# An adaptive-LayerNorm block with sliding attention: the order of work in the first group of tokens

## The chip, the core and the metric

The kernel runs on one core of a Trainium2 chip. The core has five engines with a queue each: TensorE (PE, matrix multiplication; its weight loads are shown as PEld), VectorE (DVE), ScalarE (ACT), GpSimd (POOL) and SyncE (SP), which issues transfers here. An engine works through its queue in order, and an instruction waits for the semaphores of those that it depends on. The metric is the device time of one execution, in microseconds (us).

## What is computed

A block with batch 1, 2048 tokens of 448 features, 16 heads of 28 features, and attention over a window of 256 tokens. `c` gives six vectors by way of `w_mod` (shift, scale and gate for each half).

```python
mod = (_silu(c) @ w_mod).reshape(c.shape[0], 6, 1, -1)     # sa, ca, ga, sb, cb, gb
h = _layernorm(x) * (1 + ca) + sa
q, k, v = (h @ wqkv), split over 16 heads
scores = einsum("bhqd,bhkd->bhqk", q, k) * (Dh ** -0.5)
mask = (idx[:, None] - idx[None, :] >= 0) & (idx[:, None] - idx[None, :] < 256)
o = softmax(where(mask, scores, -1e9)) @ v
x = x + ga * (o @ wo)
h = _layernorm(x) * (1 + cb) + sb
x = x + gb * (mish(h @ w1 + b1) @ w2)
```

All is in float32. The kernel writes each operand of its large products as a high part, rounded to TensorE's faster format (float32r), and a remainder, and adds the products of high with high, high with remainder and remainder with high (`passes`, L183): 11 matmuls for a projection tile of 448 features.

## The kernel before

**Groups and tiles.** The tokens are worked through in four groups of 512. For a group the projections give seven tiles of 128 features for queries and keys (`qk` tiles 0 to 6: queries are features 0 to 447, keys 448 to 895, so tile 3 holds the last queries and the first keys) and four tiles of 128 tokens for values (`v0` to `v3`). Head h has its queries at feature 28h and its keys at 448 + 28h: heads 0 and 1 of group 0 need tiles 0 and 3, heads 2 and 3 need tile 4 as well, head 4 is the first that needs tile 1, head 6 the first that needs tile 5.

**A qk tile's way.** After its 11 matmuls ScalarE copies the high part out of PSUM into a tile `st` (`hi` in `qk_out`, L314), VectorE writes the remainder beside it (`lo`, L317), and SP stores both to a scratch tensor `scr` in DRAM in two transfers, 512 KB and 256 KB (four smaller ones for tile 3, which is cut at the border between queries and keys; `put`, L322). From there `L(i)` (L563) loads the queries and keys of one head, 84 rows each, as `q` and `k`. A value tile is copied to `v` by ScalarE and VectorE in the same way (`v_out`, L331).

**Attention of a head.** `A(i, t)` (L572) forms the scores of 128 queries in the tile `sA`, and VectorE adds the mask and takes the row maxima (`mx`, L581). `M2` (L585) transposes the maxima of a pair of heads (`mt`), and SP writes them as two further rows into `q` (`q<-mr`). `B` (L601) computes scores less maxima (`sB`), of which ScalarE takes the exponential twice (`P`, `Ph`); GpSimd subtracts for the remainder `Pl` (`SP`, L626), and `PV` (L632) multiplies with `v`. `EV`, `E`, `E2` and `E3` transpose and divide.

**What sets the order.** The program is written out by hand under a manual schedule: the order of the Python calls is the order on every queue. At the start (L365 to L407) the first group is normalised and transposed, ScalarE splits the weights in three sets of columns `QCOLS` (tiles 0, 3, 4; values; tiles 1, 2, 5, 6), with the remainders on GpSimd, VectorE and GpSimd, and tiles 0, 3 and 4 are formed together, in three rounds that follow the chunks of the transposed input as these come. Then come constants on GpSimd (L412 to L439): the mask, `fdf`, the fixed columns of `V`, and the rows 64 to 85 of the six `k` buffers. L899 to L916 are the lead of the attention: the loads of heads 0 to 3, all four value tiles with tiles 1 and 5 on the way, the load of head 4, and then the maxima of heads 0 to 2, with pieces of tiles 2 and 6 and the next group's normalisation between them. The loop from L919 runs three units per head: each has a piece of `B`, of `PV` and of `A` three heads ahead, the load of a head five ahead, and a share of the other work (`fill_main`, L836: the rest of the projections and the next group's), measured out by `RATE` (L872). `fill_side` (L855) is worked off one step a unit: the next group's normalisation, then the gate and the weights `wo`.

Of the kernel before, what the change touches and what calls it, by code (L numbers as in the profile page):

```python
# [8 lines left out]
F32 = mybir.dt.float32  # L9
# [42 lines left out]
def adaln_block(ctx: ExitStack, tc: tile.TileContext, x, wqkv, wo, w1, b1, w2, c, w_mod, out):  # L52
# [4 lines left out]

    def dma(o, i):
        nc.sync.dma_start(o, i)
# [11 lines left out]
    mid, mid_s = pool("mid")  # L71
    vp, vp_s = pool("vp")
    st0, st0_s = pool("st0")
    vq, vq_s = pool("vq", side="right")
# [232 lines left out]

    def qk_out(g, m, p, st=None):
        st = st or qk.tile([128, 2, GT], F32R, name=f"st{g}_{m}", tag="qs", bufs=3)
        r0, gs = m * 128, slice(g * GT, (g + 1) * GT)  # L310
        qn = min(max(D - r0, 0), 128)

        def hi():
            ACT.activation(st[:, 0], p, AF.Copy)  # L314

        def lo():
            DVE.tensor_tensor(st[:, 1], p, st[:, 0].bitcast(F32), op=ALU.subtract)  # L317

        def store():
            later.append(put)  # L320

        def put():  # L322
            for a, b, pa, ph in ((0, qn, 0, 2), (qn, 128, 1, 0)):
                if a < b:
                    dma(scr[r0 + a:r0 + b, pa:pa + 2, gs], st[a:b].bitcast(F32))
                    dma(scr[r0 + a:r0 + b, ph, gs], st[a:b, 0].bitcast(F32))
            done.add((g, m))

        return hi, lo, store
# [18 lines left out]
    def gen_qkv(g, tiles):  # L348
        first = {"v2": ("sB", 2), "v3": ("sB", 2), 1: ("pv", 1), 5: ("tr", 1)} if g == 0 else {}
        for m in tiles:  # L350
            p = bank(*first.get(m, ("mm", 2)), f"qk{g}_{m}")
            if isinstance(m, str):
# [46 lines left out]
    for lo_n, hi_n in ((0, 3), (3, 6), (6, 11)):  # L399
        for m, p, ps in first:  # L400
            for n in range(lo_n, hi_n):
                PE.matmul(p, ps[n][1], ps[n][0], start=(n == 0), stop=(n == 10))  # L402
# [8 lines left out]
    identr = att.tile([128, 128], BF16, name="identr")  # L411
    mask = att.tile([128, 384], F32, name="mask")  # L412
# [3 lines left out]
    POOL.affine_select(mask, mask, pattern=[[-1, 384]], compare_op=ALU.is_ge, fill=NEG, base=W,  # L416
                       channel_multiplier=1)
    fdf = att.tile([128, 512], F32, name="fdf", tag="P", bufs=3)
    POOL.memset(fdf[:, 0:256], 0.0)
# [4 lines left out]
    fdmask = att.tile([128, 256], BF16, name="fdmask")  # L424
    for v in V:
        POOL.memset(v[:, :, 28:29].bitcast(F32), 1.0)
        POOL.memset(v[:, :, 29:32].bitcast(F32), 0.0)
    Q2 = [att.tile([86, 2, GT], F32R, name=f"q2_{i}") for i in range(NQ // 2)]
    Q3 = [Q2[i // 2][:, i % 2] for i in range(NQ)]
    K3 = []  # L430
    for i in range(NK):
        t = att.tile([86, GT + W], F32R, name=f"k3_{i}")
        POOL.memset(t[64:86, :].bitcast(F32), -1.0)
        K3.append(t)
    O2 = []
# [435 lines left out]

    RATE = {0: 0.48, 1: 0.88, 2: 0.88, 3: 0.62}  # L872
    FRONT = {0: 0, 1: 2, 2: 2, 3: 2}
# [17 lines left out]
    def load_slot(i):  # L891
# [5 lines left out]
        L(i)  # L897

    for i in range(LEAD + 1):  # L899
        load_slot(i)  # L900
    need({f"v{t}" for t in range(4)}, 0)
    load_slot(LEAD + 1)
    DVE.tensor_copy(identr, ident)
    DVE.tensor_copy(fdmask, fdf[:, 0:256])
    for i in range(LEAD):
        for t in range(4):
            A(i, t)
            if t % 2:
                pipe.step()
                next(fillers[0])  # L910
                flush()
            side_step(0)
        if i % 2:
            pipe.step()
            next(fillers[0])
            M2(i // 2)  # L916
    NU = 3 * NS
    credit = 0.0
    for u in range(NU + 9):  # L919
# [27 lines left out]
        if g < NG:  # L947
# [21 lines left out]
        if 0 <= u - 2 < NU:  # L969
            PV(u - 2, Ph)  # L970
    for st in (FW["s2"], att_s, vp_s):
        st.close()
# [94 lines left out]
```

## Time and profile before

| what | value |
|---|---|
| median of 3 runs (lowest, highest) | 746.62 us (741.92, 748.72) |
| the profiled execution | 747.11 us |
| its span, from the first to the last instruction | 745.3 us |
| mean granted TensorE clock over the span | 0.982 of full speed |
| busy: PE, PEld | 697.2, 592.7 us |
| busy: DVE, ACT, POOL | 374.4, 388.6, 329.7 us |
| transfers | 83.86 MB, mean 113 GB/s |

A row of the timeline reads: start, time, engine, line, operation, result<-operands, shapes, count, and in brackets how long the engine had been idle before and what ended that. `SPq` is SP's queue, where a row is the issue of a transfer, not the transfer. A row of the stages reads: the stretch, its length, for each engine the busy time and the number of instructions, then the granted TensorE clock, the share of the transfer engines and GB/s. A row of the waits reads: who waited at which line for whom, the sum in us, how often, and the longest.

### The profile page before, as it was taken

To read this page: it belongs to the slowest core of one execution; us is meant where nothing else is said; L and a number is where in the kernel's file an instruction comes from. 1 tells how busy PE (TensorE), PEld (TensorE's weight loads), DVE (VectorE), ACT (ScalarE), POOL (GpSimd) and SP (SyncE) were. 2 spreads that over 40 slices of the span, in tenths; PEclk is the share of its full clock that TensorE was granted. 3 is DMA by queue.
4 is the path that set the end of the run, shared out by engine and by line. 5 is a ranking of instruction groups with operands and counts; after the bars stand their busy time and mean duration, and the time that the engine had idled before them with its cause. 6 is when DMAs were issued, how large, how long until landed. Compare 5 with 4: busy or idle time off the path is not lost.

```text
span 745.3 us, 11923 instructions
## 1 busy us (share of the span) xinstructions
PE 697.2 (94%) x3969; PEld 592.7 (80%) x3969; DVE 374.4 (50%) x1009; ACT 388.6 (52%) x740; POOL 329.7 (44%) x358
## 2 busy tenths in 40 slices
PE   3988979999999999999989889999999999999996
PEld 3766768789779887888878678888888888888885
DVE  4768645586755587664558923242323232413113
ACT  4416767676767675766868694334223222332221
POOL 4714787677656585676768865431100000000000
PEclk9898999999999999999999999999999999999999
DMA  8667643264374364453466246510200020001001
GB/s 215 201 223 230 169 152 111 84 209 148 114 219 129 99 220 144 127 156 118 133 203 207 64 147 189 139 47 1 100 0 1 1 99 1 1 0 50 1 0 50
DMA packets 48121, 83.86 MB, mean 113 GB/s; under 512 B 6126, under 2 KB 26108, under 8 KB 48060
## 3 DMA queue, kind: packets, MB, share of 16 engines
q1 hardware_dynamic: 48060, 83.10, 36.5%
q8 instruction: 32, 0.52, 0.3%
q14 instruction: 29, 0.24, 0.1%
HBM read 53.45 MB, written 29.36 MB: 111 GB/s over the span
## 4 chain that ended last, share of the span: by engine, by line
PE 80%; DVE 7%; DMA 5%; issue 3%; ACT 3%; POOL 1%; SPq 0%; DVEq 0%; ACTq 0%; POOLq 0%
PE z L812 19%; PE pv L640 9%; PE qk L294 7%; PE acc L989 6%; PE acc L990 6%; PE acc L988 6%; PE sA L579 5%; PE wo L294 5%; PE qk_v L294 5%; PE sB L609 4%; PE sB L620 3%; DMA k<-scr 2%; DVE junk L581 2%; PE qk L402 1%; PE et L651 1%
## 5 line engine op out<-in xcount | busy, mean ns | idle before, releaser
L630 POOL TENSOR_TENSOR Pl<-P,Ph 128x512 fp32r<-128x512 f32 (+2 forms) x192 | 235.7, 1234 | 99.4 <-ACT Ph L624 64.4
L581 DVE CUSTOM_DVE_ANT_0 junk<-sA,mask 128x384 f32<-128x384 f32 (+2 forms) x256 | 135.1, 528 | 120.6 <-PE sA L579 117.2
L623 ACT ACTIVATE P<-sB 128x512 f32<-128x512 f32 (+2 forms) x192 | 109.8, 572 | 62.1 <-PE sB L620 60.0
L820 DVE TENSOR_TENSOR al<-t,ah 128x512 fp32r<-128x512 f32 x56 | 38.8, 692 | 198.4 <-ACT ah L819 198.4
L818 ACT ACTIVATE t<-z,b1c 128x512 f32<-128x512 f32 x56 | 38.6, 689 | 177.2 <-PE z L812 166.3
L579 PE MATMUL sA<-k,q 84*128 84x384 f32 (+2 forms) x256 | 102.2, 403 | 10.0 <-DMA k<-scr 4.9
L624 ACT ACTIVATE Ph<-sB 128x512 fp32r<-128x512 f32 (+2 forms) x192 | 109.3, 569 | 0.0
L812 PE MATMUL z<-hhf,w 128*128 128x512 f32 x224 | 89.4, 399 | 0.0
L812 PE MATMUL z<-hlf,w 128*128 128x512 f32 x224 | 88.7, 396 | 0.0
L640 PE MATMUL pv<-Ph,v 128*60 128x256 f32 (+2 forms) x352 | 77.6, 294 | 6.9 <-ACT o L645 6.6
L988 PE MATMUL acc<-w2h,ah 128*128 128x448 f32 x224 | 82.2, 367 | 0.0
L989 PE MATMUL acc<-w2l,ah 128*128 128x448 f32 x224 | 82.0, 366 | 0.0
L990 PE MATMUL acc<-w2h,al 128*128 128x448 f32 x224 | 81.9, 366 | 0.0
L609 PE MATMUL sB<-q,k 86*128 86x256 f32 (+1 forms) x352 | 75.4, 288 | 4.4 <-DMA q<-mr 3.7
L640 PE MATMUL pv<-Pl,v 128*60 128x256 f32 (+2 forms) x352 | 74.4, 286 | 1.3 <-POOL Pl L630 1.0
L609 PEld LDWEIGHTS sB<-q,k 86*128 86x128 f32 x352 | 62.4, 192 | 6.6 <-DMA q<-mr 2.6
L812 PE MATMUL z<-hhf,w1l 128*128 128x512 f32 x168 | 66.4, 395 | 0.0
L640 PEld LDWEIGHTS pv<-Ph,v 128*60 128x60 f32 x352 | 45.4, 134 | 23.3 <-ACT o L645 10.3
L579 PEld LDWEIGHTS sA<-k,q 84*128 84x128 f32 x256 | 50.2, 197 | 16.8 <-DVE mx L581 9.1
L620 PE MATMUL sB<-fdmask,identr 128*128 128x128 bf16 (+1 forms) x320 | 60.9, 256 | 0.0
L640 PEld LDWEIGHTS pv<-Pl,v 128*60 128x60 f32 x352 | 45.6, 133 | 10.4 <-POOL Pl L630 3.3
L645 ACT ACTIVATE o<-pv 60x512 f32<-60x512 f32 x64 | 37.8, 591 | 27.4 <-PE pv L640 26.8
(149 smaller groups left out, 1251.4 us busy)
## 6 DMA issues: line engine op xcount, KB each, us to landing
scr<-st SPq DMA_DIRECT2D x24, 512.0 KB
k<-scr SPq DMA_DIRECT2D x48, 252.0 KB
q<-scr SPq DMA_DIRECT2D x64, 168.0 KB
scr<-st SPq DMA_DIRECT2D x32, 256.0 KB
x<-x1d SPq DMA_DIRECT2D x10, 448.0 KB
xin<-in_A_x_dram SPq DMA_DIRECT2D x8, 448.0 KB
xr<-in_A_x_dram SPq DMA_DIRECT2D x16, 224.0 KB
x1d<-xr SPq DMA_DIRECT2D x16, 224.0 KB
```

Of the source, the lines that this page charges most:

```text
L294: PE.matmul(p, b, a, start=(n == 0), stop=(n == 10))
L579: PE.matmul(p[:, c0:384], q[0:84, t * 128:(t + 1) * 128], k[0:84, t * 128 + c0:t * 128 + 384], start=True, stop=True)
L581: DVE.tensor_tensor_reduce(out=junk[:, c0:384], in0=p[:, c0:384], in1=mask[:, c0:384], scale=1.0, scalar=-3.0e38, op0=ALU.add, op1=ALU.max ...
L609: PE.matmul(p[:, c:c + 128 * (t1 - t0)], k[:, jj * 128:(jj + 1) * 128], q[:, t0 * 128:t1 * 128], start=(n == 0), stop=False, skip_group_ch ...
L623: ACT.activation(P[:, c0:], p[:, c0:], AF.Exp, scale=SCALE)
L624: ACT.activation(Ph[u][:, c0:], p[:, c0:], AF.Exp, scale=SCALE)
L630: POOL.tensor_tensor(Pl[u][:, c0:], Pt[u][:, c0:], Ph[u][:, c0:].bitcast(F32), op=ALU.subtract)
L640: PE.matmul(pv[0:60, t0 * 128:t1 * 128], V[j % NV][:, h, :], P[u][:, c:c + 128 * (t1 - t0)], start=(P is Ph and b == 0 and n == 0), stop=F ...
L812: PE.matmul(zb[n], ps[m][1], ps[m][0], start=(m == 0), stop=(m == 10))
L988: PE.matmul(p, ah[n][:, ts], w2h[f], start=(f == 0), stop=False)
L989: PE.matmul(p, ah[n][:, ts], w2l[f], start=False, stop=False)
L990: PE.matmul(p, al[n][:, ts], w2h[f], start=False, stop=(f == NF - 1))
```

## The change

The names in the rows below are tiles of the program with a buffer number; line numbers of the changed kernel are up to seven higher. In both kernels the first 652 rows of TensorE's queue hold the same instructions, in another order; from the next row on the queues read alike, and so do those of the other engines from about there.

**Tiles.** Tiles 0 and 3 are formed first, in three rounds, then tile 4 by itself. The third set of weight columns is split between the two, the remainders of its first two chunks on GpSimd and of the others on VectorE. Tile 3's four stores are issued from ScalarE's queue. Tile 4's `st` is taken from the three rotating buffers instead of a place of its own. The later tiles of group 0 all take the two rotating PSUM banks `mm`; before, `v2`, `v3` and tiles 1 and 5 had other banks.

ScalarE's queue before, from the second set of weight columns to the first value tile:

```order
L164 ACTIVATE wq_96<-wqs_101 128x448
L164 ACTIVATE wq_96<-wqs_98 128x512
L164 ACTIVATE wq_96<-wqs_99 128x512
L164 ACTIVATE wq_96<-wqs_100 128x512
L164 ACTIVATE wq_96<-wqs_101 128x512
L314 ACTIVATE st_0_291<-qk_0_255 128x512
L314 ACTIVATE st_3_296<-qk_3_256 128x512
L314 ACTIVATE st_4_303<-qk_4_257 128x512
L336 ACTIVATE v_137<-qk_v_389 128x16x28
```

ScalarE's queue now, at the same place:

```order
L165 ACTIVATE wq_99<-wqs_104 128x448
L315 ACTIVATE st_0_314<-qk_0_290 128x512
L315 ACTIVATE st_3_319<-qk_3_291 128x512
L59 DMA scr<-st_3_319 64x2x512
L59 DMA scr<-st_3_319 64x512
L59 DMA scr<-st_3_319 64x2x512
L59 DMA scr<-st_3_319 64x512
L165 ACTIVATE wq_99<-wqs_101 128x512
L165 ACTIVATE wq_99<-wqs_102 128x512
L165 ACTIVATE wq_99<-wqs_103 128x512
L165 ACTIVATE wq_99<-wqs_104 128x512
L315 ACTIVATE st_4_346<-qk_4_334 128x512
```

The copies of tiles 0 and 3 and the four stores moved ahead of the last four copies of weights (128x512), and tile 4's copy stands behind these.

SP's queue before, from the last store of tile 3 to the loads of head 2:

```order
L59 DMA scr<-st_3_296 64x512
L59 DMA scr<-st_4_303 128x2x512
L59 DMA scr<-st_4_303 128x512
L59 DMA q_0_350<-scr 84x512
L59 DMA k_0_353<-scr 84x512
L59 DMA q_0_350<-scr 84x512
L59 DMA k_1_355<-scr 84x512
L59 DMA q_1_351<-scr 84x512
L59 DMA k_2_357<-scr 84x512
```

SP's queue now, from tile 0's stores to the loads of head 4, the first of the last two rows:

```order
L59 DMA scr<-st_0_314 128x512
L59 DMA scr<-st_4_346 128x2x512
L59 DMA scr<-st_4_346 128x512
L59 DMA q_0_365<-scr 84x512
L59 DMA k_0_239<-scr 84x512
...
L59 DMA k_3_245<-scr 84x512
L59 DMA q_0_365<-mr_486 1x8x128 x2
L59 DMA scr<-st_1_498 128x2x512
L59 DMA scr<-st_1_498 128x512
L59 DMA q_2_367<-scr 84x512
L59 DMA k_4_247<-scr 84x512
```

Tile 3 is gone from this queue, tile 4's stores still stand ahead of the loads of head 0, and the load of head 4 now stands behind the maxima of the first pair.

**Constants.** The fills of the six `k` buffers, the mask and the fixed columns of `V` are written on GpSimd ahead of the third set's remainders, in a pool of their own (`kq`), no longer behind them; `fdf` stays behind.

**The lead.** The load of head 4 comes after the maxima of heads 0 to 2. After six steps of the filling work (two value tiles) every `A(i, t)` of these three heads is followed by one step more; the side work starts with the loop. `RATE` of group 0 is 0.58, before 0.48. TensorE's queue before, at the first maxima, with tile 5 ahead of them:

```order
L294 MATMUL qk_5_459<-hl_223,wq_96 128x512
L579 MATMUL sA_0_480<-k_0_353,q_0_350 128x128
L579 MATMUL sA_1_487<-k_0_353,q_0_350 128x256
L294 MATMUL qk_2_491<-hh_222,wq_96 128x512
L294 MATMUL qk_2_491<-hh_222,wql 128x512
L294 MATMUL qk_2_491<-hl_223,wq_96 128x512
L294 MATMUL qk_2_491<-hh_222,wq_96 128x512
L579 MATMUL sA_2_499<-k_0_353,q_0_350 128x384
L579 MATMUL sA_3_505<-k_0_353,q_0_350 128x384
```

TensorE's queue now, at the first maxima, with the second value tile ahead of them:

```order
L295 MATMUL qk_v_407<-wq_99,hl_226 128x448
L586 MATMUL sA_0_421<-k_0_239,q_0_365 128x128
L295 MATMUL qk_v_425<-wq_99,hh_225 128x448
L295 MATMUL qk_v_425<-wql,hh_225 128x448
L295 MATMUL qk_v_425<-wq_99,hl_226 128x448
L295 MATMUL qk_v_425<-wq_99,hh_225 128x448
L586 MATMUL sA_1_430<-k_0_239,q_0_365 128x256
L295 MATMUL qk_v_425<-wql,hh_225 128x448
```

The first `sA` moved ahead of two value tiles and of tiles 1 and 5 (from row 120 to row 76 of TensorE's queue), and three or four matmuls of a projection stand between one `sA` and the next.

The diff:

```diff
-    def dma(o, i):
-        nc.sync.dma_start(o, i)
+    def dma(o, i, q=nc.sync):
+        q.dma_start(o, i)
@@
+    kq, kq_s = pool("kq")
@@
-    def qk_out(g, m, p, st=None):
-        st = st or qk.tile([128, 2, GT], F32R, name=f"st{g}_{m}", tag="qs", bufs=3)
+    def qk_out(g, m, p, q=nc.sync):
+        st = qk.tile([128, 2, GT], F32R, name=f"st{g}_{m}", tag="qs", bufs=3)
@@
-                    dma(scr[r0 + a:r0 + b, pa:pa + 2, gs], st[a:b].bitcast(F32))
-                    dma(scr[r0 + a:r0 + b, ph, gs], st[a:b, 0].bitcast(F32))
+                    dma(scr[r0 + a:r0 + b, pa:pa + 2, gs], st[a:b].bitcast(F32), q)
+                    dma(scr[r0 + a:r0 + b, ph, gs], st[a:b, 0].bitcast(F32), q)
@@
     def gen_qkv(g, tiles):
-        first = {"v2": ("sB", 2), "v3": ("sB", 2), 1: ("pv", 1), 5: ("tr", 1)} if g == 0 else {}
         for m in tiles:
-            p = bank(*first.get(m, ("mm", 2)), f"qk{g}_{m}")
+            p = bank("mm", 2, f"qk{g}_{m}")
@@
-    x_load(1)
-    for c0, c1 in QCOLS[1:]:
-        for ci in range(4):
-            split_hi(wqs[ci][:, c0:c1], wq3[:, ci, c0:c1], ACT)
-    for (c0, c1), eng in zip(QCOLS[1:], (DVE, POOL)):
-        for ci in range(4):
-            split_lo(wqs[ci][:, c0:c1], wq3[:, ci, c0:c1], wql[:, min(ci, 2), c0:c1], ci, eng)
-    first = [(m, bank(tag, b, f"qk0_{m}"), qk_passes(0, m)) for m, tag, b in ((0, "pv", 1), (3, "tr", 1), (4, "sA", 2))]
-    for lo_n, hi_n in ((0, 3), (3, 6), (6, 11)):
-        for m, p, ps in first:
-            for n in range(lo_n, hi_n):
-                PE.matmul(p, ps[n][1], ps[n][0], start=(n == 0), stop=(n == 10))
-    for m, p, ps in first:
-        st = st0.tile([128, 2, GT], F32R, name="st0_4") if m == 4 else None
-        for f in qk_out(0, m, p, st):
-            f()
-        flush()
-    st0_s.close()
-    att, att_s = pool("att")
+    K3 = []
+    for i in range(NK):
+        t = kq.tile([86, GT + W], F32R, name=f"k3_{i}")
+        POOL.memset(t[64:86, :].bitcast(F32), -1.0)
+        K3.append(t)
+    mask = kq.tile([128, 384], F32, name="mask")
+    for v in V:
+        POOL.memset(v[:, :, 28:29].bitcast(F32), 1.0)
+        POOL.memset(v[:, :, 29:32].bitcast(F32), 0.0)
+    x_load(1)
+
+    def split_cols(c0, c1, engs):
+        for ci in range(4):
+            split_hi(wqs[ci][:, c0:c1], wq3[:, ci, c0:c1], ACT)
+        for ci in range(4):
+            split_lo(wqs[ci][:, c0:c1], wq3[:, ci, c0:c1], wql[:, min(ci, 2), c0:c1], ci, engs[ci])
+
+    split_cols(*QCOLS[1], (DVE, DVE, DVE, DVE))
+
+    def first_tiles(tiles):
+        for lo_n, hi_n in ((0, 3), (3, 6), (6, 11)):
+            for m, p in tiles:
+                ps = qk_passes(0, m)
+                for n in range(lo_n, hi_n):
+                    PE.matmul(p, ps[n][1], ps[n][0], start=(n == 0), stop=(n == 10))
+        for m, p in tiles:
+            for f in qk_out(0, m, p, nc.scalar if m == 3 else nc.sync):
+                f()
+            flush()
+
+    first_tiles([(0, bank("pv", 1, "qk0_0")), (3, bank("tr", 1, "qk0_3"))])
+    split_cols(*QCOLS[2], (POOL, POOL, DVE, DVE))
+    first_tiles([(4, bank("sA", 2, "qk0_4"))])
+    st0_s.close()
+    att, att_s = pool("att")
@@
-    RATE = {0: 0.48, 1: 0.88, 2: 0.88, 3: 0.62}
+    RATE = {0: 0.58, 1: 0.88, 2: 0.88, 3: 0.62}
@@
+    def fill0():
+        pipe.step()
+        next(fillers[0])
+        flush()
+
     for i in range(LEAD + 1):
         load_slot(i)
-    need({f"v{t}" for t in range(4)}, 0)
-    load_slot(LEAD + 1)
     DVE.tensor_copy(identr, ident)
     DVE.tensor_copy(fdmask, fdf[:, 0:256])
+    for _ in range(6):
+        fill0()
     for i in range(LEAD):
         for t in range(4):
             A(i, t)
-            if t % 2:
-                pipe.step()
-                next(fillers[0])
-                flush()
-            side_step(0)
+            fill0()
         if i % 2:
-            pipe.step()
-            next(fillers[0])
             M2(i // 2)
+    load_slot(LEAD + 1)
@@
-            if v > 1:
+            if v > 1 or g == 0:
                 side_step(g)
```

More of the change, by code (lines that the diff above doesn't have):

```diff
@@ L390, in adaln_block @@
         hT_lo(trs[ci], ci, hh, hl)
-    x_load(1)
-    for c0, c1 in QCOLS[1:]:
-        for ci in range(4):
-            split_hi(wqs[ci][:, c0:c1], wq3[:, ci, c0:c1], ACT)
-    for (c0, c1), eng in zip(QCOLS[1:], (DVE, POOL)):
-        for ci in range(4):
-            split_lo(wqs[ci][:, c0:c1], wq3[:, ci, c0:c1], wql[:, min(ci, 2), c0:c1], ci, eng)
-    first = [(m, bank(tag, b, f"qk0_{m}"), qk_passes(0, m)) for m, tag, b in ((0, "pv", 1), (3, "tr", 1), (4, "sA", 2))]
-    for lo_n, hi_n in ((0, 3), (3, 6), (6, 11)):
-        for m, p, ps in first:
-            for n in range(lo_n, hi_n):
-                PE.matmul(p, ps[n][1], ps[n][0], start=(n == 0), stop=(n == 10))
-    for m, p, ps in first:
-        st = st0.tile([128, 2, GT], F32R, name="st0_4") if m == 4 else None
-        for f in qk_out(0, m, p, st):
-            f()
-        flush()
-    st0_s.close()
-    att, att_s = pool("att")
-    identr = att.tile([128, 128], BF16, name="identr")
-    mask = att.tile([128, 384], F32, name="mask")
+    K3 = []
[4 more added lines that the diff above has]
+    mask = kq.tile([128, 384], F32, name="mask")
     POOL.memset(mask, 0.0)
@@ L417, in adaln_block @@
                        channel_multiplier=1)
+    for v in V:
[23 more added lines that the diff above has]
+    att, att_s = pool("att")
+    identr = att.tile([128, 128], BF16, name="identr")
     fdf = att.tile([128, 512], F32, name="fdf", tag="P", bufs=3)
@@ L424, in adaln_block @@
     fdmask = att.tile([128, 256], BF16, name="fdmask")
-    for v in V:
-        POOL.memset(v[:, :, 28:29].bitcast(F32), 1.0)
-        POOL.memset(v[:, :, 29:32].bitcast(F32), 0.0)
     Q2 = [att.tile([86, 2, GT], F32R, name=f"q2_{i}") for i in range(NQ // 2)]
     Q3 = [Q2[i // 2][:, i % 2] for i in range(NQ)]
[L430 to L434, printed above, removed]
     O2 = []
@@ L970, in adaln_block @@
             PV(u - 2, Ph)
-    for st in (FW["s2"], att_s, vp_s):
+    for st in (FW["s2"], att_s, kq_s, vp_s):
         st.close()
```

## The prediction

> **What bounds the kernel now.** I read the page's first part, then TensorE's busy time and granted clock stage by stage, then who kept TensorE waiting, then the start of the program in order of time.
>
> ```profile
> span 745.3 us, 11923 instructions
> PE 697.2 (94%) x3969; PEld 592.7 (80%) x3969; DVE 374.4 (50%) x1009; ACT 388.6 (52%) x740; POOL 329.7 (44%) x358
> ...
> core 0: us, PE busy (x) PEld busy (x) DVE busy (x) ACT busy (x) POOL busy (x), PEclk, DMA share, GB/s
> 43.00:59.00 16.00, 11.82 (x55) 7.91 (x53) 13.16 (x46) 2.85 (x6) 2.23 (x6) 1.00 0.64 214
> 59.00:67.00 8.00, 7.33 (x31) 5.95 (x32) 6.42 (x17) 4.39 (x10) 3.69 (x4) 0.57 0.63 213
> 67.00:97.00 30.00, 25.91 (x168) 20.16 (x167) 18.24 (x61) 22.11 (x50) 23.57 (x24) 1.00 0.67 190
> 97.00:101.00 4.00, 3.80 (x16) 3.16 (x17) 1.38 (x7) 0.66 (x2) 2.91 (x4) 0.57 0.09 33
> 101.00:133.00 32.00, 30.94 (x215) 25.82 (x213) 18.27 (x73) 25.23 (x59) 24.70 (x27) 1.00 0.46 142
> ...
> PE sA L579 <- DMA k<-scr: 3.3, 1, 3.3
> PE sA L579 <- DVE mx L581: 2.9, 6, 0.9
> PE tr L232 <- DVE hl L243: 1.2, 1, 1.2
> PE sB L609 <- DMA q<-mr: 1.1, 2, 0.6
> PE mt L587 <- DVE mx L581: 0.8, 2, 0.4
> PE pv L640 <- POOL Pl L630: 0.5, 1, 0.5
> PE tr L232 <- POOL Pl L630: 0.3, 1, 0.3
> ```
>
> TensorE is busy for 94% of the span, so time can be won only where it waits or runs at a low clock. The change does not alter its work: the first 652 rows of its queue are the same instructions in another order, and from the next row on both queues read alike. So I count losses between 43 and 133 us, where that point lies. The five stages hold 94 us minus 79.8 busy; of the 90 us from 43 to 133 that leaves 10.2 idle (16+8+30+4+32 less 11.82+7.33+25.91+3.80+30.94), and the waits listed add up to 10.1. Two stages ran at a mean clock of 0.57 and lost 7.33 x 0.43 = 3.15 and 3.80 x 0.43 = 1.6. Old losses: 10.2 + 4.8 = 15.0 us. That is the most the change can win.
>
> **The change: the start.** What decides is when the first maxima (tile sA of head 0) can run.
>
> ```profile
> 22.63 4.15 POOL L170 TENSOR_TENSOR wql<-wqs,wq 128x512 fp32r<-128x512 f32 x3 [4.51 <-ACT wq L164]
> 23.96 4.94 DVE L170 TENSOR_TENSOR wql<-wqs,wq 128x448 fp32r<-128x448 f32 x3
> 24.01 0.63 ACT L164 ACTIVATE wq<-wqs 128x512 fp32r<-128x512 f32 x1 [0.66 <-DMA wqs<-in_A_wqkv_dram]
> 27.48 0.60 ACT L314 ACTIVATE st<-qk 128x512 fp32r<-128x512 f32 x1 [1.66 <-PE qk L402]
> 28.93 0.62 DVE L172 TENSOR_TENSOR wq<-wqs,wq 64x448 fp32r<-64x448 f32 x1
> 29.59 1.89 DVE L317 TENSOR_TENSOR st<-qk,st 128x512 fp32r<-128x512 f32 x3
> 29.61 0.36 PE L294 MATMUL qk_v<-wq,hh 128*128 128x448 f32 x1
> 30.31 6.88 SPq L59 DMA_DIRECT2D scr<-st  x8
> 32.63 4.15 POOL L433 MEMSET k<- 22x768 f32 x6
> 38.70 0.39 PE L294 MATMUL qk<-hh,wq 128*128 128x512 f32 x1
> 40.56 0.99 POOL L438 MEMSET o<- 32x512 f32 x2 [3.78 <-DMA scr<-st]
> 43.82 0.40 PE L579 MATMUL sA<-k,q 84*128 84x128 f32 x2
> ...
> 49.94 0.89 SPq L59 DMA_DIRECT2D scr<-st  x2
> 51.21 0.55 DVE L581 CUSTOM_DVE_ANT_0 junk<-sA,mask 128x384 f32<-128x384 f32 x1
> 53.90 1.53 SPq L59 DMA_DIRECT2D q<-mr  x2
> 56.70 0.41 PE L609 MATMUL sB<-q,k 86*128 86x384 f32 x1 [0.61 <-DMA q<-mr]
> 89.08 2.85 SPq L59 DMA_DIRECT2D scr<-st  x4
> 92.97 0.45 SPq L59 DMA_DIRECT2D k<-scr  x1
> 97.20 0.45 PE L579 MATMUL sA<-k,q 84*128 84x128 f32 x1 [3.25 <-DMA k<-scr]
> 100.79 0.81 SPq L59 DMA_DIRECT2D q<-scr  x1
> 101.30 0.59 ACT L645 ACTIVATE o<-pv 60x512 f32<-60x512 f32 x1 [1.06 <-PE pv L640]
> 133.55 0.59 ACT L645 ACTIVATE o<-pv 60x512 f32<-60x512 f32 x1
> ```
>
> Today 44 matmuls of the v tiles run from 29.61 to 38.70 (0.207 each), then the 22 of tiles 1 and 5 until 43.82 (0.233 each); only then come the maxima, with their keys long there. In the changed order TensorE does two v tiles, 22 x 0.207 = 4.5 us, and stands before sA of head 0 at 29.61 + 4.5 = 34.15.
>
> When are its keys there? Tile 4 now follows, so tile 3 ends 11 x 0.233 = 2.6 us earlier, at 27.05. ScalarE takes over 0.2 later (today tile 0 ends ten matmuls ahead of 29.61, at 27.28, and its copy starts at 27.48) and copies for 0.60: 27.85. VectorE takes the rest, 1.89 / 3 = 0.63: 28.5. Now ScalarE issues its four stores. No row shows a store issued there. The nearest is the same four stores on SP at 89.08, 2.85 us; below it stands half of the 0.89 row per store, 1.8; above it 6.88 / 8 per store, 3.4. I take 2.85: 31.4. Behind these stand four copies of the last weight columns, 4 x 0.63: 33.9, the third at 33.3. VectorE does two of their remainders: beside GpSimd's, as in the row at 23.96, 4.94 / 3 = 1.65 each; alone 0.62. I take one of each, since GpSimd has two of its own (4.15 / 3 = 1.4 each from 32.0 on) and is done at about 35: 35.6. Then tile 4's remainder, 0.63: 36.3. Only now can SP issue tile 4's two stores (0.89), and head 0's loads stand behind them on SP: q 0.81, so the keys' load is issued at 38.1. The row at 92.97 was 4.2 us from issue to use behind other traffic; the second of the two small loads at 53.90 (issued about 54.7) took 2.0. I take 3.6, because 768 KB of tile 4 go ahead: 41.7.
>
> So TensorE waits at 34.15 until 41.7: **7.5 us** that it does not wait today (bounds 3.9, with every low value above, and 9.1, with every high one). Such a wait takes the clock too: the 3.25 us at 97 were followed by 1.6 us lost, the broken stretch 43 to 59 by 3.15. I take **2.4**, the middle, and keep both ends.
>
> [...]
>
> Constants sooner: cost nothing. GpSimd sat idle for 4.51 us before 22.63, and the six fills of k (4.15) with the mask and the v columns now fill that gap; its next work, the weight remainders, waits for ScalarE anyway. No load waits for a k fill: today's end at 32.63 + 4.15 = 36.8, ahead of the first load. Tile 3 on the scalar queue takes half of SP's 6.88 us away, but SP then waits for tile 4, so it wins nothing on the path. What is queued behind the stores on ScalarE is counted above. VectorE casts fdmask ahead of the first v tile's remainder, and fdmask is built on GpSimd behind the weight remainders, done at about 35; the third v tile needs that bank. The wait until 41.7 hides this; with the keys in time it would hold TensorE for about 2 us. Tile 4's st in the rotating buffers only makes tile 2 wait for a store that ended long before. RATE and the later steps of the side work move the same instructions to later units: nothing, with TensorE the bound there (30.94 of 32).
>
> **The maxima among projections.** The waits of sA and mt for VectorE, 2.9 + 0.8, go: between two sA now stand three or four matmuls, 0.7 to 0.9 us, against 0.55 for the widest maximum. The 3.3 at 97.20 with its 1.6 of clock go as well in my count: there the keys of head 10 were queued on SP behind the four stores at 89.08; the row that now stands behind these stores belongs to head 13, three heads after the preceding pair's maxima instead of two. The waits tr for VectorE (1.2), sB for the maxima's load (1.1) and those for Pl (0.8) stay: 3.1.
>
> What is late next: head 4, whose queries need tile 1. From the end of tile 1, at T: copy 0.6 and remainder among the maxima, about T+2.9; stores issued, 0.89, T+3.8; finished 3.3 later as today (last issue ends at 30.31 + 6.88 = 37.2, o waits for it until 40.56): T+7.1, for which SP waits; two loads issued, 0.8, and 2.0 to land: T+9.9. TensorE has 19 matmuls of 0.233 and 21 smaller ones (about 0.13, just under the 30.94 / 215 of the last stage) until it wants these keys, T+7.2, and the wait for the first pair's maxima, 0.5. That makes **2.3 us** of new wait (0 to 4) and 0.8 of clock (0 or 1.6).
>
> **Sum.** New losses 7.5 + 2.4 + 2.3 + 0.8 + 3.1 = 16.1 against 15.0: +1.1 us. The profiled execution took 747.11, 0.5 above the median of the three runs, 746.62; +1.1 is well inside what these terms leave open, and I put the changed kernel at **747.0**.
>
> **Rivals.**
> Loads in time (faster). If ScalarE's stores are quick and the queue is empty, the keys land when TensorE arrives, and the first wait and its clock fall away and at most the 2 us for the v bank come: 16.1 - 9.9 + 0 to 2 = 6.2 to 8.2, 7 to 9 us less, about 738.5. For it: the transfer engines are idle between tile 3's stores and tile 4's. Against it: SP's order puts tile 4's stores first, and even the low bounds leave 3.9. It decides from a wait under about 1.5 us.
> A chain of late loads (slower). SP works in order, and the loads of heads 4 and 6 both wait for a store's completion behind another pair's maxima. If each costs what 97.20 did (3.3 and 1.6), the losses are 7.5 + 2.4 + 2 x 4.9 + 3.1 = 22.8: +7.8, 755. For it: 7.1 us from a tile's end to a stored tile, and then the loads, against 9.2 of work between such heads (the o copies of heads 6 and 13, at 101.30 and 133.55, stand seven heads apart, 4.6 each). Against it: there is one such wait in today's 90 us. It decides from 10 us between a tile's end and its keys.
> The maxima are not covered after all: the 3.7 us for VectorE stay, since it also does statistics and remainders there: +4.8, 751.5.
>
> **How the numbers follow.** Chances: my forecast 0.58, the uncovered maxima 0.12, loads in time 0.16, the chain 0.14. All low bounds together give 3.9 + 1.6 + 0 + 0 + 3.1 = 8.6, 6.4 less, 740.2; the loads in time go below that, the chain to 755. The range 739.5 to 754 leaves out the greater part of both. A measurement of this kernel tells about 1% from no change, 7.5 us, and the forecast and the uncovered maxima lie inside that: faster 0.16, same 0.70, slower 0.14.
>
> **What would show it.** In the changed profile sA of head 0 should wait for k<-scr for 4 to 9 us from about 34, with half clock behind it, and SP should issue tile 4's stores at 35 to 38. The waits of sA for mx should be under 1 us in all, and the one at 97 gone. Wrong would be a first sA before 36, tile 4's stores on SP before 33, or waits for k<-scr that come back with every second head.

## The result and the profile after

| | before | changed |
|---|---|---|
| median of 21 runs each | 744.99 us | 745.35 us |
| lowest, highest | 741.11, 749.5 | 743.13, 748.52 |
| ratio, 95% interval | 1 | 1.001 (0.9992 to 1.0028) |
| the profiled execution, its span | 747.11, 745.3 us | 747.5, 745.7 us |
| mean granted TensorE clock | 0.982 | 0.985 |

The change makes no difference that this measurement can tell from none. A second measurement of the unedited changed kernel (E12 below) gave 1.0028 (1.0001 to 1.0055): if there is a loss, it is at most about half a percent.

First the page of the changed kernel, then the stage from 34 to 43 in the kernel before, where it was filled with work, then the stages of the changed kernel:

```profile
span 745.7 us, 11913 instructions
PE 694.2 (93%) x3969; PEld 591.8 (79%) x3969; DVE 374.4 (50%) x1011; ACT 388.2 (52%) x740; POOL 326.9 (44%) x356
```

```profile
34.00:43.00 9.00, 9.00 (x43) 7.76 (x42) 2.79 (x6) 2.23 (x4) 3.77 (x7) 1.00 0.93 260
```

```profile
34.00:43.00 9.00, 0.13 (x1) 0.00 (x0) 4.18 (x6) 2.13 (x5) 4.33 (x7) 0.68 0.49 141
43.00:59.00 16.00, 14.66 (x68) 12.62 (x68) 9.16 (x34) 3.05 (x6) 0.00 (x0) 0.86 0.29 93
59.00:67.00 8.00, 5.85 (x31) 4.67 (x30) 5.44 (x20) 3.88 (x9) 4.07 (x5) 0.85 0.40 132
67.00:97.00 30.00, 27.14 (x177) 21.27 (x175) 25.06 (x71) 21.04 (x47) 20.09 (x25) 0.98 0.69 222
97.00:101.00 4.00, 4.00 (x31) 3.45 (x30) 2.61 (x10) 3.26 (x8) 2.83 (x3) 1.00 0.43 100
101.00:133.00 32.00, 31.17 (x203) 25.15 (x202) 16.99 (x69) 24.92 (x58) 29.40 (x30) 1.00 0.61 183
```

The stages from 67 on are better than before (27.14 against 25.91 busy, 4.00 at full clock against 3.80 at 0.57, 31.17 against 30.94), and the broken stretch from 43 to 59 is closed (14.66 against 11.82). It is paid for between 34 and 43, where TensorE does 0.13 us of work, by a clock of 0.86 and 0.85 behind that, and by a second wait between 59 and 67 (5.85 us busy). The waits of TensorE between 20 and 135 us say the same:

```profile
PE sA L586 <- DMA k<-scr: 12.4, 2, 10.2
PE qk L420 <- ACT hh L388: 1.5, 1, 1.5
PE pv L647 <- ACT o L652: 1.2, 1, 1.2
PE tr L233 <- DVE hl L244: 0.9, 1, 0.9
PE pv L647 <- POOL Pl L637: 0.8, 2, 0.7
PE tr L233 <- DVE xin L223: 0.5, 1, 0.5
```

The rows of sA and mt for mx are gone, and so is the 3.3 us wait at 97. In their place stand two waits for keys, 12.4 us together. (The wait for hh, 1.5, lies ahead of the first value tile.) The chain behind the longer one, in order of time, from the timeline of ScalarE (ACT, ACTq), VectorE, SP and TensorE:

```profile
27.06 0.60 ACT L315 ACTIVATE st<-qk 128x512 fp32r<-128x512 f32 x1 [0.57 <-PE qk L420]
28.77 3.76 ACTq L59 DMA_DIRECT2D scr<-st  x4
32.58 2.20 ACT L165 ACTIVATE wq<-wqs 128x512 fp32r<-128x512 f32 x4 [4.92 <-DMA scr<-st]
35.17 1.65 DVE L173 TENSOR_TENSOR wq<-wqs,wq 64x512 fp32r<-64x512 f32 x1
36.84 0.69 DVE L318 TENSOR_TENSOR st<-qk,st 128x512 fp32r<-128x512 f32 x1
37.56 0.87 SPq L59 DMA_DIRECT2D scr<-st  x2
38.53 0.84 SPq L59 DMA_DIRECT2D q<-scr  x1
39.55 0.44 SPq L59 DMA_DIRECT2D k<-scr  x1
44.34 0.44 PE L586 MATMUL sA<-k,q 84*128 84x128 f32 x1 [10.21 <-DMA k<-scr]
63.85 0.30 PE L586 MATMUL sA<-k,q 84*128 84x128 f32 x1 [2.15 <-DMA k<-scr]
```

Read it from the bottom up. Head 0's first sA waits 10.21 us for a load that SP issues at 39.55. SP reaches that load only after tile 4's stores at 37.56, these wait for tile 4's remainder at 36.84, and this stands on VectorE behind a remainder of the weights, which waits for ScalarE, and ScalarE is held for 3.76 us by tile 3's four stores (0.65, 0.62, 1.75 and 0.62 us: it is the third that takes long). The last row is head 4.

One number serves to compare kernels: the time from the first matmul of a value tile to ScalarE's copy of head 15's result. In both kernels 611 recorded matmuls lie in it, and what the start takes before it (which moved by 3 us between profiled executions of these kernels, whatever the edit) is left out. First the kernel before, then the changed one; the columns are those of the stages:

```profile
29.61:145.46 115.85, 104.87 (x611) 83.90 (x609) 69.22 (x234) 66.62 (x150) 74.01 (x104) 0.96 0.55 169
```

```profile
29.43:147.39 117.96, 101.40 (x611) 82.67 (x609) 70.98 (x234) 68.65 (x154) 71.03 (x78) 0.94 0.54 165
```

The stretch grew by 2.1 us: idle time rose from 10.98 to 16.56, and busy time for the same matmuls fell from 104.87 to 101.40. Busy time falls too when the clock is higher: in the changed kernel a matmul of 448 columns starts 0.37 to 0.38 us after the one before it at half clock (45.06 to 46.18) and 0.20 us after it at full clock (47.90 to 48.30). Outside the stretch there is noise of its own: what comes behind it took 594.5 to 602.0 us in the fourteen profiled executions.

### The profile page after: what moved, and what is told of

Its sections match the earlier page's. It is cut to its first block, busy times and chain, and to the rows that moved or that the text cites. A ratio compares the mean times of both kernels' runs of the same rounds, so it can differ in the third digit from the quotient of the medians.

```text
span 745.7 us, 11913 instructions
## 1 busy us (share of the span) xinstructions
PE 694.2 (93%) x3969; PEld 591.8 (79%) x3969; DVE 374.4 (50%) x1011; ACT 388.2 (52%) x740; POOL 326.9 (44%) x356
## 4 chain that ended last, share of the span: by engine, by line
PE 76%; DMA 7%; DVE 7%; ACT 3%; issue 3%; SPq 2%; POOL 1%; DVEq 0%; ACTq 0%; POOLq 0%
PE z L819 19%; PE pv L647 9%; PE qk L295 7%; PE acc L996 6%; PE acc L997 6%; PE acc L995 6%; PE sA L586 5%; PE sB L616 4%; PE qk_v L295 4%; PE wo L295 4%; DMA k<-scr 3%; PE sB L627 3%; DVE junk L588 2%; SPq L59 2%; DMA wm<-in_w_mod_dram 1%
```

## The experiments

**Theory.** What the lead wins (the waits for maxima, the wait at 97, half clock there) is given back in one wait of head 0 for its keys, whose length is set by the order of issue: tile 3's stores on ScalarE, the weights behind them, tile 4, tile 4's stores on SP, head 0's loads behind these. **Rivals:** the wait is set by the transfers themselves; the second queue helps; the clock behind the wait costs nothing; or the time is set by something that no wait of TensorE shows.

All results at a glance. The ratio is to the kernel before, run on the same chip, with its 95% interval; the stretch is the one defined above, from one profiled execution (for E3 one that lies 8 us above its median). Only E11 ran beside the changed kernel itself (as E12); elsewhere a comparison with the changed kernel is one of two ratios.

| | kernel | ratio | stretch, us | first sA's wait |
|---|---|---|---|---|
| | before | 1 | 115.9 | none |
| | changed | 1.001 (0.9992–1.0028) | 118.0 | 10.2 |
| E1 | loads of heads 0, 1 ahead of tile 4's stores | 0.9947 (0.992–0.9974) | 112.2 | 4.3 |
| E2 | tile 3's stores on SP | 0.9968 (0.9944–0.9993) | 114.2 | 5.9 |
| E3 | twelve steps ahead of the maxima | 1.0074 (1.0047–1.01) | 123.4 | none |
| E4 | 36 idle matmuls in the wait | 0.9995 (0.9966–1.0025) | 115.0 | 0.5 |
| E5 | new lead, old start | 1.0044 (1.0018–1.0071) | 115.9 | 8.0 |
| E6 | old lead, new start | 0.9972 (0.9946–0.9999) | 114.5 | none |
| E7 | E3 with side work in the lead | 1.0041 (1.0014–1.0067) | 119.6 | none |
| E8 | E1 with tile 1 sooner | 0.9937 (0.9907–0.9967) | 108.8 | 3.4 |
| E9 | E8, tile 3's keys stored first, on SP | 0.9897 (0.9856–0.9938) | 107.2 | 1.4 |
| E10 | E9 with these stores on ScalarE | 0.9887 (0.9852–0.9922) | 106.0 | 1.2 |
| E11 | E5 again | 1.0028 (1.0–1.0056) | 116.7 | 8.3 |
| E12 | changed, again | 1.0028 (1.0001–1.0055) | 118.6 | 9.8 |

**E1: the order on SP.** The first loop stands behind tiles 0 and 3, ahead of tile 4.

```diff
-    acc01 = st0.tile([112, 2 * D], F32, name="acc01")
+    acc01 = wm01[0]
@@
+    q2_0 = kq.tile([86, 2, GT], F32R, name="q2_0")
@@
+    for h in range(2):
+        f0, f1 = h * DH, D + h * DH
+        dma(q2_0[0:84, h].bitcast(F32), scr[f0:f0 + DH, :, 0:GT].rearrange("d a n -> (d a) n"))
+        dma(K3[h][0:84, W:].bitcast(F32), scr[f1:f1 + DH, :, 0:GT].rearrange("d a n -> (d a) n"))
@@
-    for i in range(LEAD + 1):
+    for i in range(2, LEAD + 1):
```

The first pair's queries need a place sooner, and the sum `acc01` is formed in place to make room for it.

> The loads of heads 0 and 1 are issued on SP as soon as tiles 0 and 3 are stored, ahead of tile 4's two stores. Theory (the order on SP holds the keys back): ScalarE's stores of tile 3 are issued by 32.5 and finished about 35, so the keys of head 0 are issued about 36 where it was 39.55, with nothing in front of them, and land in 2 to 3 us instead of 4.8. The first sA runs at 38 to 40, not at 44.3, its wait falls from 10.2 to 4 to 6 us, and the time falls by 4 to 6 us, to about 740. Rival (the transfers themselves are slow, whatever the order): the wait stays above 8 us, or tile 4's stores, now behind four loads, come late and heads 2 and 3 wait by as much; time unchanged within 1.5 us. Rival (the time is set elsewhere, by work that no wait of TensorE shows): the wait is shorter and the time the same.

Measured: 740.32 us, ratio 0.9947. SP and TensorE in its timeline:

```profile
33.12 0.38 SPq L59 DMA_DIRECT2D q<-scr  x1
36.31 0.32 SPq L59 DMA_DIRECT2D k<-scr  x1
...
38.34 0.90 SPq L59 DMA_DIRECT2D scr<-st  x2
39.01 0.45 PE L591 MATMUL sA<-k,q 84*128 84x128 f32 x1 [4.29 <-DMA k<-scr]
59.73 0.30 PE L591 MATMUL sA<-k,q 84*128 84x128 f32 x1 [2.26 <-DMA k<-scr]
```

Counted from the first matmul of a value tile, the keys are issued 3.8 us sooner (6.29 us behind it, not 10.12) and used 2.7 us after that instead of 4.8; the wait falls to 4.29 and the stretch by 5.7 us. Heads 2 and 3 do not pay for it. Of the 5.9 us, 2.1 are won behind the issue, where the load no longer follows tile 4's 768 KB. Both rivals fall: the order of issue set the wait, and the wait set the time.

**E2: the queue of tile 3's stores.**

```diff
-            for f in qk_out(0, m, p, nc.scalar if m == 3 else nc.sync):
+            for f in qk_out(0, m, p, nc.sync):
```

> Tile 3's four stores go back to SP, behind the two of tile 0; the rest of the changed kernel stays. Theory (ScalarE held by its own stores delays the weights, these tile 4, and tile 4's stores the keys): ScalarE goes on with the weights at 29, not at 32.6; tile 4's stores are ready about 34, and SP, which needs 6.9 us x 6/8 = 5.2 for six stores from 28 on, is free at about 33.5. The first wait falls from 10.2 to 6.5 to 8 us and the time by 2 to 3.5 us, to about 742.5. Rival (the second queue pays): SP becomes the late one, the first wait is 10 us or more and the time rises by 0 to 3 us.

Measured: 743.0 us, ratio 0.9968. Its timeline of SP (eight stores of tiles 0, 3 and 4, then a load) and of ScalarE and TensorE:

```profile
30.19 6.07 SPq L59 DMA_DIRECT2D scr<-st  x8
36.36 1.19 SPq L59 DMA_DIRECT2D q<-scr  x1
37.66 0.50 SPq L59 DMA_DIRECT2D k<-scr  x1
```

```profile
29.21 0.60 ACT L315 ACTIVATE st<-qk 128x512 fp32r<-128x512 f32 x1 [0.56 <-PE qk L420]
29.71 2.19 ACT L165 ACTIVATE wq<-wqs 128x512 fp32r<-128x512 f32 x4
42.14 0.44 PE L586 MATMUL sA<-k,q 84*128 84x128 f32 x1 [5.86 <-DMA k<-scr]
```

ScalarE goes from tile 3's copy straight to the weights, where the changed kernel has a gap of 4.92, and the wait is 5.86, somewhat below what was expected. Moving the stores to the scalar queue, one part of the change, made the wait longer: the second queue relieved SP, which then had to wait for tile 4 all the same, and held for 3.76 us the engine whose work tile 4 needs.

**E3 and E7: filling the wait with the group's own work.** E3 is `range(12)` for `range(6)` in the lead.

> Twelve steps of the filling work (all four value tiles) stand ahead of the first maxima, not six. Theory (the wait is time without work for TensorE, and any work put there is won): the 22 matmuls of two value tiles, 4.5 us, fill the wait, which falls from 10.2 to about 5.7; the time falls by 4 to 5 us, to about 741. Rival (the keys come later when the value tiles use ScalarE and SP first, or the same work is missed between the maxima): the wait falls, but waits of sA for mx come back (3.7 us as in the kernel before) and the time falls by less than 1.5 us.

Measured: 750.6 us, ratio 1.0074: a miss, with the sign wrong. (The rows of its profiled execution are read for where the waits stand, not for their sum.) The first three waits of TensorE:

```profile
PE tr L233 <- DVE xin L223: 6.0, 1, 6.0
PE qk_v L295 <- DVE v L340: 3.4, 1, 3.4
PE sA L586 <- DMA k<-scr: 2.5, 1, 2.5
```

The first sA does not wait for its keys any more; the wait for keys in the last row is head 10's, at 104. But the third value tile waits 3.4 us for a bank, which VectorE empties only behind the constants' casts and tile 4's remainder, and at 58 TensorE has used up the group's projections and stands before the next group's transposes, whose normalisation begins with the loop. E7 was made to test that reading; behind each maximum of the lead it takes one step of the side work:

```diff
             A(i, t)
             fill0()
+            side_step(0)
@@
-            if v > 1 or g == 0:
+            if v > 1:
                 side_step(g)
```

> The kernel of the twelve steps, with one step of the side work (the next group's normalisation) behind every maximum of the lead, as in the kernel before. It was 5 us slower than the changed kernel though its wait for keys was 2.5 instead of 12.4. Theory (the twelve steps used the group's own projections up, so that the next group's transposes came at 58 while its normalisation, which starts with the loop, ended at 64): the 6.0 us wait of tr for xin falls under 1.5, its clock comes back, and the time falls by 5 to 8 us against the twelve steps, to 743 to 746; the 3.4 us wait for a bank (qk_v for v) stays. Rival (the filling work is missed later, whatever the normalisation does): another wait of 3 us or more stands between 58 and 100 and the time stays above 748.

Measured: 748.07 us, ratio 1.0041.

```profile
PE sA L586 <- DMA k<-scr: 6.8, 2, 4.3
PE qk_v L295 <- DVE v L340: 4.5, 1, 4.5
PE qk L420 <- ACT hh L388: 1.5, 1, 1.5
```

The wait of tr for xin is gone, as the theory said, but only 2.5 us came of it where 5 to 8 were expected. Half of the rival holds: the keys of head 4 now come late, 4.3 us, since the side work put three loads of `w_mod` and the filling work the stores of tiles 5 and 2 ahead of their load on SP. Work moved into a wait has to come from somewhere, and its transfers come along.

**E4: the clock behind the wait.**

```diff
+    dummy = bank("sB", 2, "dummy")
+    hh0 = HT[0][0]
+    for _ in range(36):
+        PE.matmul(dummy, hh0[:, 0, 0:128], hh0[:, 0], start=True, stop=True)
```

> 36 further matmuls of 512 columns, whose result nobody uses, stand ahead of the first sA: extra work of 36 x 0.21 = 7.6 us, inside the 10.2 us of waiting. Theory (a long wait also costs clock behind it): the wait shrinks to about 2.5 us, the granted clock stays at 1.00 from 34 to 47 instead of the half clock of 37.4 to 47.2, and the time falls by the clock's part alone, 1.5 to 2.5 us, to about 743.3. Rival (the half clock after the wait costs nothing, because the maxima or the keys of the next heads set the pace there): clock at 1.00, time unchanged within 1 us.

Measured: 743.93 us, ratio 0.9995. The stages from 34 to 67:

```profile
34.00:43.00 9.00, 9.00 (x42) 7.57 (x41) 4.22 (x6) 2.50 (x6) 4.76 (x7) 1.00 0.52 156
43.00:59.00 16.00, 15.46 (x81) 13.00 (x80) 10.65 (x38) 3.86 (x9) 1.47 (x2) 1.00 0.35 115
59.00:67.00 8.00, 5.91 (x31) 4.65 (x30) 4.38 (x18) 3.60 (x9) 4.18 (x6) 0.80 0.47 161
```

The clock stays at 1.00 through the former wait, and the stretch is 3.0 us shorter in these two executions, though part of that is ScalarE's four stores, which took 3.07 here and not 3.76: the first sA stands 13.38 us behind the first matmul of a value tile and not 14.91, which is 1.5 of the 3.0. The other 1.5 come behind the first sA, where the changed kernel ran at half clock. The measured times differ by 1.4 us with intervals that overlap. The half clock is shown to hang on the wait; its price, 1.5 to 2.5 by the theory and 0 by the rival, is 1.5 in this pair of executions and not settled in the end time.

**E5, E11 and E12: the lead alone.** E5 is the kernel before with the new lead, its `RATE` and its banks.

> The kernel before with the new lead alone (six steps of the filling work, then the maxima of three heads with a step between each two, the load of head 4 last, RATE 0.58, side work from the loop on); its start with three tiles at once and all stores on SP stays. Theory (the lead brings the gain and the first wait alike, the start only sets how long it is): TensorE stands before the first sA at about 34; SP issues head 0's loads at 37.2 as in the kernel before, so the keys are there at 40.5 to 42 and the wait is 6 to 8 us, 3 less than the 10.2 of the changed kernel; the waits of sA for mx and the one at 97 are gone; about 742. Rival (the lead needs the new start): the first wait is 10 us or more, or other waits come, and the time is 745 or above.

Measured: 748.42 us, ratio 1.0044, where 742 was expected. The first wait came out at the upper end of what was expected, and the waits for maxima are gone:

```profile
PE sA L578 <- DMA k<-scr: 10.2, 2, 8.0
PE qk L401 <- ACT hh L387: 1.5, 1, 1.5
```

Since time and profile disagreed, it was run again beside the changed kernel.

> The new lead on the start of before once more, beside the changed kernel on the same chip, since its time (748.4) and its profile (head 13 two microseconds sooner after the first value tile than in the changed kernel) disagree. Theory (the first wait sets the time; its 8.0 us instead of 10.2 must show): 2 to 3 us below the changed kernel. Rival (the old start costs something that the first wait does not show): 2 to 3 us above it, as measured.

> The changed kernel itself, unedited, as the other side of that comparison: 745 to 746, level with the kernel before within 0.3%, by every theory.

Measured: 746.86 and 745.34 us, both at a ratio of 1.0028. So the lead without the new start is as slow as with it: the lead brings gain and wait alike. The stretch is 1.9 to 2.1 us shorter than in the changed kernel in both pairs of executions, and the end times do not show it. Behind the stretch the same kernel took 600.4 us in E5 and 594.8 in E11, so single executions can't show 2 us at the end, and the intervals (0.28% is 2.1 us) can't either. Whether something outside the stretch eats the gain stays open.

**E6: the start alone.** The changed kernel with the lead, the banks and the `RATE` of the kernel before.

> The changed kernel with the lead of the kernel before (four value tiles, tiles 1 and 5 first, in their former banks, then the maxima; RATE 0.48). Theory (the new start by itself brings nothing, since TensorE does not get to the keys before 43): the first wait is 0 to 1.5 us, the waits of sA for mx (2 to 4 us in all) and the long one near 97 (3 us) are back, head 4's is gone; the time is that of the kernel before within 2 us, 743 to 747. Rival (the start itself saves time: constants sooner, a second queue): 742 or less.

Measured: 743.45 us, ratio 0.9972.

```profile
PE sA L587 <- DVE mx L589: 3.0, 6, 0.9
PE sA L587 <- DMA k<-scr: 2.9, 1, 2.9
PE mt L595 <- DVE mx L589: 0.7, 2, 0.4
```

The old waits are back one for one, at 3.0, 2.9 and 0.7 where the kernel before has 2.9, 3.3 and 0.8, and the long wait is gone. The new start by itself is worth 2.1 us, with 0 to 4 inside the interval; the lead, on this start, costs what it wins and about 3 to 4 us more, by the two ratios of the changed kernel.

**E8, E9 and E10: a version that beats both.** E8 is E1 with tile 1 formed ahead of the last two value tiles.

```diff
-            yield from gen_qkv(0, VT + (1, 5, 2, 6))
+            yield from gen_qkv(0, VT[:2] + (1,) + VT[2:] + (5, 2, 6))
```

> The kernel with the loads of heads 0 and 1 ahead of tile 4's stores, and tile 1 formed before the last two value tiles. Theory (head 4 waits because tile 1's store is finished too late): tile 1's stores are issued ahead of the first pair's maxima, before 48, the loads of head 4 right behind these, and the wait of 2.2 us at head 4 is gone; 2 to 3 us less than without, about 738. Rival (another thing is late next: the last value tiles for PV, or tile 5 for head 6): a wait of 1.5 us or more appears there and the time stays at 740.

Measured: 739.62 us, ratio 0.9937. In its waits k<-scr stands once, 3.4 us, for head 0; head 4's 2.26 of E1 is gone, and the stretch is 3.4 us shorter, of which 0.9 are the first wait's. The medians differ by 0.7 us, with intervals wider than the difference, so the end time alone does not show this step.

E10 changes E8 further: tile 3's two stores of keys come first, on ScalarE, its two of queries behind the loads of heads 2 and 3 on SP, and the casts of `identr` and `fdmask` behind the maxima of head 0. E9 is the same with all of these stores on SP.

```diff
-            for a, b, pa, ph in ((0, qn, 0, 2), (qn, 128, 1, 0)):
-                if a < b:
+            for a, b, pa, ph in ((qn, 128, 1, 0), (0, qn, 0, 2)):
+                if g == 0 and m == 3 and a == 0:
+                    late.append((st, qn))
+                elif a < b:
@@
+    for st, qn in late:
+        dma(scr[384:384 + qn, 0:2, 0:GT], st[0:qn].bitcast(F32))
+        dma(scr[384:384 + qn, 2, 0:GT], st[0:qn, 0].bitcast(F32))
@@
-    DVE.tensor_copy(identr, ident)
-    DVE.tensor_copy(fdmask, fdf[:, 0:256])
     for _ in range(6):
         fill0()
     for i in range(LEAD):
         for t in range(4):
             A(i, t)
             fill0()
+        if i == 0:
+            DVE.tensor_copy(identr, ident)
+            DVE.tensor_copy(fdmask, fdf[:, 0:256])
```

> A version meant to be better than both. To the kernel with the early loads and tile 1 ahead of the last value tiles: tile 3's two stores of keys stand right behind tile 0's two on SP, the two of queries (needed from head 13 on) behind the loads of heads 0 to 3, and VectorE's two casts of constants behind the first maxima. Theory (the keys of head 0 wait for the whole of tile 3, issued in 3.2 to 3.8 us on ScalarE): half of the bytes are stored ahead of the load, the keys' load is issued 2 us sooner, the first wait falls from 3.4 to 1 to 2 us; ScalarE is free 3 us sooner, so tile 4 is stored sooner too; 1 to 3 us less, about 737.5. Rival (four stores in a row on SP are held as ScalarE's were): the keys' load is no sooner and the time the same as without, 739 to 741.

> The same, with the two stores of keys on ScalarE. Theory: two stores there take 1.0 to 1.3 us of ScalarE, without the third that was held for 1.75 us; the keys' load is issued 2 us sooner, the first wait is 1 to 2 us; 737 to 738. Rival (the transfers' finishing, not their issue, sets the wait): first wait above 2.5 us and 739 to 741. If both orders come out alike, the second queue is worth nothing here.

Measured: 736.29 us (0.9897) and 735.63 us (0.9887). E10's rows of ScalarE, SP and TensorE, and its stretch:

```profile
28.73 1.31 ACTq L59 DMA_DIRECT2D scr<-st  x2
33.01 0.32 SPq L59 DMA_DIRECT2D k<-scr  x1
35.61 0.30 PE L595 MATMUL sA<-k,q 84*128 84x128 f32 x1 [1.21 <-DMA k<-scr]
```

```profile
29.74:135.78 106.04, 98.90 (x611) 80.07 (x609) 71.60 (x234) 68.78 (x154) 71.01 (x78) 1.00 0.58 180
```

The wait is 1.2 us (1.4 in E9), the clock 1.00 throughout, and the stretch 9.8 us shorter than before: the kernel is 1.1% faster than the kernel before, and by the ratios as much faster than the changed one. Of the wait that is left, the rows show where it comes from: the stores are issued by 30.04, the load, which depends on them, at 33.01, and the keys are used 2.6 us later. Which of the three edits that E10 adds to E8 is worth how much was not tried. Which queue issues the two stores makes no difference that the intervals show. That the time of issue can lie in the wrong queue, E2 shows: a first wait of 5.86 us with tile 3's four stores on SP, of 10.21 with them on ScalarE.

## Why the prediction was right, and where it was off

Forecast 747.0 us (739.5 to 754.0), from a sum of +1.1 us; measured 745.35, +0.4. The stretch grew by 2.1 in one pair of executions. (In the sum, the five stages hold 90 us, not 94; the 10.2 us of idle time are right.) The mechanism, gains given back in the first wait, is shown by E1, E2, E6 and E10. The terms one by one:

- **The first wait, 7.5 (3.9 to 9.1): too small, outside its bounds.** This is the mis-sized term. TensorE arrived at 44.34 - 10.21 = 34.13, as worked out (34.15), and tile 3's copy began at 27.06 (27.25). Its own high values, two remainders of 1.65 among them, add up to 9.7 and not to 9.1; 10.2 lies above both. Off were two durations: ScalarE's stores took 3.76 where the row from SP gave 2.85, and the first keys took 4.8 from issue to use where 3.6 was taken. With smaller delays on ScalarE, VectorE and SP between them, the load was issued at 39.55, not 38.1. The bound of 3.4 for the stores came from SP's eight at 0.86 each, and four on ScalarE took 0.94 each; no row showed a load right behind tile 4's 768 KB. In the seven other profiled executions with four stores on ScalarE they took 3.07 to 3.81 us.
- **Clock, 2.4 + 0.8 = 3.2: right in sum, not one by one.** The half clock lasted from 37.25 to 47.49 and from 64.56 to 67.97. TensorE was at work in the end of the first stretch and in all of the second:

```profile
44.34:47.49 3.15, 3.15 (x9) 2.88 (x10) 1.16 (x5) 0.00 (x0) 0.00 (x0) 0.50 0.68 196
64.56:67.97 3.41, 3.41 (x14) 2.81 (x13) 2.02 (x7) 1.26 (x3) 2.05 (x3) 0.50 0.27 100
```

Half of these is 1.6 for the first wait, where 2.4 was taken, and 1.7 for head 4's, where 0.8 was. Counted in the same way, the first wait cost 1.6 to 3.1 us in the seven profiled executions in which it lasted 3.4 us or more. By busy time the price is somewhat lower: the changed kernel's stretch has 101.40 busy, E10's, at a clock of 1.00 throughout, 98.90 for the same matmuls, 2.5 us less.
- **Head 4's wait, 2.3: right** (2.15), and for the reason given: E8, with tile 1's stores sooner, has it no more.
- **Waits for maxima and the wait at 97, to go: right.** E6, with the old lead, has them back.
- **Kept waits, 3.1: right in sum** (3.4 by the rows above), though not one by one: a wait of 1.2 for a copy of o is new at 82, and the wait for q<-mr fell out of the list.
- **The old losses, 15.0: too small, which made up for the first wait.** Against E10's 98.90 the kernel before has 104.87 busy, 6.0 more; the two stages at 0.57 account for 4.8. By this measure its losses in the stretch were 10.98 + 5.97 = 16.95, the changed kernel's 16.56 + 2.50 = 19.06. What the other 1.2 us are is only argued: a matmul that runs alone counts with its whole record (0.40 us for 512 columns in the kernel before), while in a dense row there, from 39.39 on, the next one starts after 0.23 us, so a broken stretch looks busier than it is.
- **Constants sooner cost nothing, but for the bank that waits for fdmask: right that the bank waits, not why.** The prediction named the long wait as the cover of that bank; E3 and E7, where the keys no longer held TensorE, show the wait at 3.4 and 4.5 us (2 was the estimate). GpSimd's work on fdf is not what is late: in the changed kernel it ends at 37.21, and VectorE goes without a gap from the last remainders of the weights (35.17) by tile 4's (36.84) to the two casts (37.45, 37.58). The bank waits behind VectorE's queue.

Of the rivals, loads in time did not come, since SP's order did put tile 4's stores first; with another order E10 came to a wait of 1.2 and fell below the 738.5 of that rival, for it removes head 4's wait as well. The chain of late loads has one link, head 4, and the maxima were covered. Two errors, 2.7 us in the first wait and 2.0 in the old losses, nearly cancelled in the sum; that the forecast missed by less than 2 us is luck in part, and better than the working behind it.

## What to carry to other kernels

When work is reordered so that an operand is wanted sooner, follow that operand back through every queue, and put its own stores and loads ahead of transfers that are wanted later, before filling the gap with other work: E1 moved four loads and won about 5 us, and E3 moved 22 matmuls and lost about 5. A store issued from a busy engine's queue costs that engine's time (3.76 us of ScalarE for four here); if what waits behind it feeds the same chain, the second queue lengthens the chain (a first wait of 10.2 us against 5.9 in E2). And compare kernels over a stretch that holds the same instructions: busy time and listed waits alone misjudged the old losses by 2 us.

## What the runs showed of the hardware

- Issue of stores was not linear here: four from ScalarE's queue took 3.07 to 3.81 us in the eight executions with four, two (E10) 1.31. In the changed kernel it is the third that takes 1.75 us, while the others take 0.62 to 0.65 each. What holds the third, no run here tells.
- The clock did not fall behind every wait. For the first sA it stayed at 1.00 from 34 on behind 1.2 and 1.4 us (E10, E9), and fell behind 3.4 and more (0.81 from 34 to 43 in E8, 0.70 in E1). Head 4's wait of 2.1 to 2.4 us was followed by a clock of 0.79 to 0.88 from 59 to 67 in five kernels or runs and by 1.00 in two, E1 and E11, where it was longest (2.26 and 2.43). Nor did a fall need one long wait: in the kernel before the clock went to 0.50 at 59.48, and the longest waits of TensorE shortly ahead of that were 0.6 us, until 56.70, and 1.2 us, until 59.41; it had been busy for 1.65 of the 3.41 us from 56.07 to 59.48. So among waits of 0.6 to 2.4 us the length of a single one did not tell whether it cost clock; what did, no run here shows.
- Half clock lasted from 59.48 to 66.31 and from 97.03 to 100.44 in the kernel before (6.83 and 3.41 us), and 10.24 and 3.41 us in the changed one (the two stretches given above).
